# Sigmoid attention with a soft mixture of experts: logits of a whole batch in one block, a last pair by token halves, another split of held-back weights

## Chip, cores, metric

One core of a Trainium2 chip. The metric is device time in microseconds (us) of one execution, the median of several; lower is better. All data are fp32 in the chip's memory (DRAM) at the start, and the output goes back there.

## What is computed

```
scores = q @ k^T / sqrt(64) - log(448)          # 8 batches x 12 heads, 448 tokens, head size 64
x      = sigmoid(scores) @ v                    # laid out as 3584 tokens x 768
logits = x @ phi                                # 32 slots: 8 experts x 4
d      = softmax of logits over the 3584 tokens
slot   = d^T @ x                                # 32 x 768
per expert e: relu(slot[e] @ w1[e]) @ w2[e]     # 768 -> 1024 -> 768
out    = softmax of logits over the 32 slots, @ slot_out
```

The softmax over tokens runs across all batches, so it is kept as a running maximum and sum, and the slot sums are rescaled as batches come in.

## The kernel before

**Pairs and groups.** Two heads that share 128 partitions are a pair (48 pairs, `NP`); two pairs are a group (24 groups, `NG`); three groups are a batch (`NQ`). The loop `for n in range(NG)` handles one group. The engines TensorE (PE), VectorE (DVE), ScalarE (ACT) and the DMA queue SP are in manual order: each runs its instructions exactly as the program is written, and an instruction that waits holds up all that stand behind it on its engine.

**A group on PE.** `qk_full` makes the scores of both pairs for the first 384 keys in three chunks each, ACT takes the sigmoid (`sigmoid`), `av_full` multiplies by V (six matmuls per pair, two heads side by side), then come the last 64 keys of both pairs (`qk_mid` of the *next* group, `av_mid` of this one). At the start of the next group `evac` copies the result from PSUM (bank pair 2) to an x tile in SBUF. There are two x tiles, used in turn.

**Logits.** For a group, `logits_job` multiplies the two pairs of the *previous* group by phi: 4 token blocks (128, 128, 96 and 96 tokens) on 4 column quarters of the array, 8 matmuls, accumulated over two pairs. DVE adds the result to `lt_all[:, b]` (`logits_add`). So a batch has three such blocks of 8 matmuls on PE. In the group with n % 3 == 0 from n = 3 on (`edge`) the block stands between the V products of the two pairs, and the softmax over tokens of the finished batch follows (`softmax_a`, `softmax_b`). In the next group (`after`) the weights `dr` that the slot sums need are spread over partitions through DRAM: DVE transposes, SP writes `zd` and reads it back as four parts `dr` (`spread`), and on PE the block of logits is followed by `slot_job`, 56 matmuls that read `dr` part by part.

**Weights.** 128 units of 384 KB (64 of w1, then 64 of w2) stream through a ring of `N_A + N_B` = 68 SBUF tiles. `N_A` = 50 tiles (`wa`) exist from the start, and are filled during attention. The other 18 (`wb`) lie where attention's tiles were, so their loads stand behind the last attention loads on SP and wait tile by tile for what lay there. All later loads reuse ring tiles.

**The last group** (`final`) has its own order: V products of the first pair, a matmul by the identity that brings `lt_all[:, 7]` into PSUM, logits of the 4 earlier pairs so far missing there (two of them), `av_mid`, V products of the last pair, logits of the two last pairs, then `last_job`.

**The experts.** For w1: `w1_part`, `h_part`; for w2 two halves of the output columns. While the second half's products run, `out_batch` makes the outputs of the first half. `N_LATE` = 16 units are held back and loaded between the stores of the first four batches (`N_MIX` = 4 times: 4 stores, then 4 units); the other stores follow all loads. After the last unit come `gather`, `sum_groups` and the second half's `out_batch`.

**Fillers.** At the start PE runs `FILL` = 37 tiny matmuls (32x8) and `WARM` = 3 of 128x128 while the first inputs load; in the second half of w2 `warm(3)` stands in four of the steps.

Of the kernel before, what the change touches and what calls it, by code (L numbers as in the profile page):

```python
# [9 lines left out]
F32 = mybir.dt.float32  # L10
F32R = mybir.dt.float32r
AF = mybir.ActivationFunctionType
ALU = mybir.AluOpType
# [3 lines left out]
B, H, S, D = 8, 12, 448, 64  # L17
# [7 lines left out]
NFC = F // P  # L25
HALF = DM // 2
UNIT = 768
GAP = 128
N_A = 50
N_B = 18  # L30
N_LATE = 16
N_MIX = 4
QW = 2 * S
NP = B * NPR
NG = B * NQ
WARM = 3
FILL = 37
WN = 128
CW = 256
NBK = 4  # L40
# [8 lines left out]
def soft_moe_attention(ctx: ExitStack, tc: tile.TileContext, qk, v, phi, w1, w2, cst, out):  # L49
# [19 lines left out]
    nc.vector.memset(acc[:, 0:256], 0.0)  # L69
    nc.vector.memset(nbias, -math.log(S))  # L70
    nc.gpsimd.memset(lt_all, NEG)

    units = [("w1", e, 2 * uu + y, kh) for e in range(E) for uu in range(2) for kh in range(2) for y in range(2)]
    units += [("w2", hf, e, g, y) for hf in range(2) for e in range(E) for g in range(2) for y in range(2)]
# [42 lines left out]
    with ExitStack() as actx:  # L117
        ldq = actx.enter_context(tc.tile_pool(name="ldq", bufs=2))
        sp = actx.enter_context(tc.tile_pool(name="sp", bufs=2))
        one = {}  # L120
        for name in ("v0", "att4", "x0", "att3", "v2", "att0", "att1", "att2", "v1", "gap"):
            one[name] = actx.enter_context(tc.tile_pool(name=f"{name}p", bufs=1))
        yp = actx.enter_context(tc.tile_pool(name="yp", bufs=1))
        one["x1"] = actx.enter_context(tc.tile_pool(name="x1p", bufs=1))
        one["gap"].tile([P, GAP], F32, name="gap")
        bounce = actx.enter_context(tc.tile_pool(name="bounce", bufs=2, space=bass.MemoryType.DRAM))
        ps = actx.enter_context(tc.tile_pool(name="ps", bufs=1, space=PSUM))

        def bank2(i):
            return ps.tile([P, 2, 512], F32, name=f"b{i}")  # L130
# [68 lines left out]
        def av_mid(n, flags):  # L199
            att, vt = atts["mid", n], vs[n, 2]  # L200
            for h, d in enumerate(heads):
                for i, r in enumerate(heads):
                    start, stop = flags[i]
                    nc.tensor.matmul(avs["p", 2 * n + i][d, 0:S], vt[r, 0, d], att[r, h, :], start=start, stop=stop)  # L204

        def new_x(n):
            xTs[n] = one[f"x{n % 2}"].tile([P, 2, S], F32, name=f"x{n % 2}")
            for i in range(2):
                xTs["p", 2 * n + i] = xTs[n][:, i, :]

# [10 lines left out]
        def logits_job(lp, pairs, first=True, last=True):  # L221
            for m, p in enumerate(pairs):
                for j in reversed(range(4)):
                    nc.tensor.matmul(  # L224
                        lp[32 * j:32 * j + 32, 0:TOK[j]], phi_sb[:, p % NPR, :],
                        xTs["p", p][:, TOF[j]:TOF[j] + TOK[j]],
                        start=(first and m == 0), stop=(last and m == len(pairs) - 1))

        def logits_add(lp, b, first):
            for r, w in ((slice(0, 64), TOK[0]), (slice(64, 128), TOK[3])):  # L230
                dst, part = lt_all[r, b, 0:w], lp[r, 0:w]
                if first:
                    nc.vector.tensor_copy(dst, part)
                else:
                    nc.vector.tensor_tensor(out=dst, in0=part, in1=dst, op=ALU.add)

        def logits(n, i):
            lp = bank2(i)[:, 0, :]
            logits_job(lp, (2 * n, 2 * n + 1))
            return lp  # L240

        def softmax_a(b):
            t1 = small.tile([P, 2, 132], F32, name="t1")
# [183 lines left out]
        for n in range(NG):  # L427
            pa, pb = 2 * n, 2 * n + 1
            bp = n // NQ - 1
            edge, after, third = (n >= NQ and n % NQ == i for i in range(3))  # L430
            final = n == NG - 1
            if third:
                load_v(n, 1)
            load_qk(pa + 2)
            load_qk(pb + 2)
            load_v(n, 2)
            if third:
                slot_evac(bp)
            if n > 0:
                evac(n - 1)  # L440
                for p in ((pa - 4, pa - 3) if third else ()) + (() if after else (pa - 2, pa - 1)):
                    turn(p)
            if after:
                softmax_r(bp)
                softmax_c(bp)
                spread(bp)
            for _ in range(weights_of(n)):
                load_unit()
            load_v(n + 1, 0)
            if not after:  # L450
                load_v(n + 1, 1)
            if third:
                combine_c(bp)
            if edge and bp > 0 or final:
                bq = bp if final else bp - 1
                combine_d(bq, dts[bq][:, 0, 0:P])
            qk_full(pa)
            split_all(pa + 2)
            qk_full(pb)
            split_all(pb + 2)  # L460
            if final:
                avs["p", pa] = bank2(2)[:, 0, :]
                av_full(pa, True, False)
                lg = bank2(0)[:, 0, 0:P]
                nc.tensor.matmul(lg, ident, lt_all[:, B - 1], start=True, stop=False)
                logits_job(lg, [NP - 4, NP - 3], first=False, last=False)
                avs["p", pb] = bank2(3)[:, 0, :]
                av_mid(n, ((False, True), (True, False)))
                new_x(n)
                xa, xb = xTs["p", pa], xTs["p", pb]  # L470
                nc.vector.tensor_copy(xa, avs["p", pa][:, 0:S])
                turn(pa)
                av_full(pb, False, True)
                logits_job(lg, [pa], first=False, last=False)
                nc.scalar.copy(xb[:, 256:S], avs["p", pb][:, 256:S])
                nc.vector.tensor_copy(xb[:, 0:256], avs["p", pb][:, 0:256])
                logits_job(lg, [pb], first=False)
                turn(pb)
                break
            avs[n] = bank2(2)  # L480
            for i in range(2):
                avs["p", pa + i] = avs[n][:, i, :]
            av_full(pa, True, False)
            if edge:
                lp = logits(n - 1, 3)
                logits_add(lp, bp, False)
                softmax_a(bp)
                softmax_b(bp)
            av_full(pb, True, False)
            if n > 0 and not edge:  # L490
                lp = logits(n - 1, 3 if after else 0)
                if after:
                    combine_b(bp)
                logits_add(lp, n // NQ, n % NQ == 1)
            if after:
                slot_job(bp)
            qk_mid(n + 1)
            av_mid(n, ((False, True), (False, True)))
# [127 lines left out]
    for i in range(2 * E):  # L626
        w2_step(po, 1, *divmod(i, 2))
        if i == 1:
            st = sum_groups(so)
        if 3 <= i < 3 + B:  # L630
            out_batch(0, i - 3, st)
            if i < 3 + N_MIX:
                store(4)
                for _ in range(N_LATE // N_MIX):
                    load_unit()
        if 2 + B <= i < 2 * E - 2:
            warm(3)
    so = gather(po)
    store(len(stores))
    st = sum_groups(so)  # L640
# [38 lines left out]
```

## Time and profile before

| what | value |
|---|---|
| time, median of 3 runs | 391.31 us (391.17 to 393.25) |
| the profiled execution | 390.81 us, of which span 389.0 us |
| granted TensorE clock, mean | 0.985 |
| busy: DVE, ACT, POOL | 58%, 49%, 1% of the span |
| share of PE in the chain that ended last | 85% |
| share of DMA in that chain | 9% |
| read from DRAM, written | 85.43 MB, 11.47 MB |

A profile is of one execution, from its first to its last instruction (the span); the time measured contains 1.8 us around it. Busy shares are means over stages with different limits, so each stage has to be read by itself: the page's slices and the stretches (windows) do that. The chain is followed back from the last instruction, at each step to what released it. The SP rows are the DMA queue: the time at which it issued a transfer, not the transfer's end.

### The profile page before, as it was taken

How to read it: one execution, taken by the hardware profiler on the slowest of the kernel's cores; microseconds unless marked ns; L12 is line 12 of the kernel's file. 1: busy time of each engine (PE TensorE's matmuls, PEld its weight loads, DVE VectorE, ACT ScalarE, POOL GpSimd, SP SyncE). 2: the span in 40 equal slices, each digit the busy share in tenths (PEclk: the TensorE clock that was granted, in tenths of full speed). 3: DMA queues.
4: the chain of work that ended last, by engine and by line, in shares of the span. 5: the costliest groups of instructions: out<-in, count | busy, mean ns of one | idle time of the engine just before them, and what ended most of it. 6: DMA issues, size and time to landing. Idle time of an engine off the chain costs nothing.

```text
span 389.0 us, 9831 instructions
## 1 busy us (share of the span) xinstructions
PE 364.2 (94%) x4058; PEld 188.8 (49%) x4058; DVE 226.5 (58%) x518; ACT 190.2 (49%) x243; POOL 3.3 (1%) x13
## 2 busy tenths in 40 slices
PE   8999999999999999999999999999989989977750
PEld 5444556554555654555554456555455543313210
DVE  3555776776887677697667777776643410420340
ACT  4656675664667456566645666564530110320240
POOL 1000000000000000000000000000020000000000
PEclk9999999999999999999999999999999999999995
DMA  7777856773784567477547755442899999999987
GB/s 212 256 245 238 285 156 192 244 255 102 244 296 144 183 227 239 161 240 244 195 137 227 274 159 203 142 150 70 294 390 387 401 399 402 383 385 374 366 287 242
DMA packets 49276, 97.54 MB, mean 251 GB/s; under 512 B 5584, under 2 KB 26704, under 8 KB 49232
## 3 DMA queue, kind: packets, MB, share of 16 engines
q1 hardware_dynamic: 49232, 96.92, 72.7%
q8 instruction: 32, 0.52, 0.6%
q14 instruction: 12, 0.10, 0.1%
HBM read 85.43 MB, written 11.47 MB: 249 GB/s over the span
## 4 chain that ended last, share of the span: by engine, by line
PE 85%; DMA 9%; DVE 2%; ACT 1%; issue 1%; SPq 0%; ACTq 0%
PE b L195 29%; PE b L176 24%; PE b L187 6%; PE px L535 6%; PE b L204 5%; DMA wb<-in_w_dram 4%; PE b L318 4%; DMA wa<-in_w_dram 3%; PE b L224 3%; PE po L601 3%; PE px L578 2%; PE px L552 1%; DMA qkt<-in_qk_dram 1%; DVE wa L583 1%; PE b L383 0%
## 5 line engine op out<-in xcount | busy, mean ns | idle before, releaser
L164 ACT ACTIVATE att<-b,nbias 128x896 f32<-128x896 f32 x168 | 158.6, 1007 | 84.7 <-PE b L187 64.7
L195 PE MATMUL b<-att,v 128*64 128x448 f32 x576 | 115.3, 545 | 0.0
L176 PE MATMUL b<-qs,ks 64*128 64x448 f32 x864 | 95.7, 372 | 0.0
L176 PEld LDWEIGHTS b<-qs,ks 64*128 64x128 f32 x864 | 77.4, 184 | 26.3 <-PE b L187 6.3
L195 PEld LDWEIGHTS b<-att,v 128*64 128x64 f32 x576 | 38.5, 136 | 61.6 <-issue 54.1
L213 DVE COPY x<-b 128x896 f32<-128x896 f32 x23 | 25.1, 1091 | 33.1 <-PE b L204 33.1
L155 DVE TENSOR_TENSOR qs<-qkt,qs 128x448 fp32r<-128x448 f32 x48 | 30.0, 625 | 1.7
L155 DVE TENSOR_TENSOR ks<-qkt,ks 128x384 fp32r<-128x384 f32 x48 | 26.8, 558 | 1.6
L219 DVE STREAM_TRANSPOSE y<-x 128x448 f32<-128x448 f32 x48 | 27.3, 617 | 0.4
L187 PE MATMUL b<-qkt 64*64 64x448 f32 x192 | 25.2, 569 | 0.3 <-DMA qkt<-in_qk_dram 0.2
L153 DVE CAST qs<-qkt 128x448 fp32r<-128x448 f32 x48 | 18.4, 384 | 9.6 <-DMA qkt<-in_qk_dram 6.5
L204 PE MATMUL b<-att,v 64*64 64x448 f32 x192 | 22.4, 537 | 0.0
L583 DVE COPY wa<-px 96x768 f32<-96x768 f32 x13 | 12.2, 952 | 13.2 <-PE px L578 13.2
L583 ACT COPY wa<-px 128x768 f32<-128x768 f32 x13 | 10.3, 799 | 17.6 <-PE px L578 14.2
L535 PE MATMUL px<-wa,sT 128*32 128x256 f32 x300 | 17.8, 381 | 0.6 <-DVE sT L386 0.6
L578 PE MATMUL px<-st,lt_all 32*128 32x384 f32 (+1 forms) x128 | 16.8, 524 | 1.5 <-DVE st L614 0.7
L318 PE MATMUL b<-y,dr 32*32 32x192 f32 x896 | 17.7, 331 | 0.2 <-ACT dr L309 0.2
L224 PEld LDWEIGHTS b<-x,phit 128*32 128x32 f32 x384 | 9.1, 109 | 17.0 <-issue 11.3
L153 DVE CAST ks<-qkt 128x384 fp32r<-128x384 f32 x47 | 16.6, 353 | 0.0
L224 PE MATMUL b<-x,phit 128*32 128x96 f32 (+1 forms) x384 | 16.0, 266 | 0.2
L614 DVE COPY st<-px 128x384 f32<-128x384 f32 x2 | 1.1, 557 | 25.4 <-PE px L612 25.4
L318 PEld LDWEIGHTS b<-y,dr 32*32 32x32 f32 x896 | 12.9, 103 | 3.4 <-issue 1.4
(131 smaller groups left out, 211.5 us busy)
## 6 DMA issues: line engine op xcount, KB each, us to landing
wa<-in_w_dram SPq DMA_DIRECT2D x98, 384.0 KB, 7.0
qkt<-in_qk_dram SPq DMA_DIRECT2D x48, 448.0 KB, 4.1
wb<-in_w_dram SPq DMA_DIRECT2D x30, 384.0 KB, 5.8
v<-in_v_dram SPq DMA_DIRECT2D x48, 192.0 KB, 2.5
out_dram<-wa SPq DMA_DIRECT2D x26, 192.0 KB, 3.4
out_dram<-wa SPq DMA_DIRECT2D x26, 144.0 KB, 3.2
dr<-zd SPq DMA_DIRECT2D x28, 64.0 KB, 2.0
v<-in_v_dram SPq DMA_DIRECT2D x24, 64.0 KB, 4.2
```

The lines of the kernel that those rows point to most:

```text
L153: copy(dst[:, 0, :], src)
L155: nc.vector.tensor_tensor(out=dst[:, 1, :], in0=src, in1=dst[:, 0, :].bitcast(F32), op=ALU.subtract)
L164: nc.scalar.activation(att[:], sc[:, :, 0:S], AF.Sigmoid, bias=nbias, scale=QSCALE)
L176: nc.tensor.matmul(sc[:, h, 0:S], ks[r, z, c * P:(c + 1) * P], qs[r, y, :], start=(z + y == 0), stop=(z == 1))
L187: nc.tensor.matmul(sc[r, h, 0:S], t[d, S + NQK:QW], t[d, 0:S], start=True, stop=True)
L195: nc.tensor.matmul(avs["p", p][r, 0:S], vs[n, i][:, c, r], atts[p, c][:, h, :], start=(start and c == 0), stop=(stop and c == NFULL - 1))
L204: nc.tensor.matmul(avs["p", 2 * n + i][d, 0:S], vt[r, 0, d], att[r, h, :], start=start, stop=stop)
L219: nc.vector.transpose(ys[b][:, hp, :], xTs["p", p])
L224: nc.tensor.matmul(lp[32 * j:32 * j + 32, 0:TOK[j]], phi_sb[:, p % NPR, :], xTs["p", p][:, TOF[j]:TOF[j] + TOK[j]], start=(first and m == ...
L318: nc.tensor.matmul(sl[a // 2][32 * j:32 * j + 32, a % 2, 0:NPR * BLK], drs[b][32 * a:32 * a + 32, j, c * BLK:(c + 1) * BLK], y[32 * a:32 * ...
L535: nc.tensor.matmul(ph[32 * j:32 * j + 32, uu, 0:256], sT[:, 3 * kh + kc, :], utile[("w1", e, 2 * uu + j // 2, kh)][:, kc * 256:(kc + 1) * ...
L583: (nc.scalar.copy if g == 0 else nc.vector.tensor_copy)(ov, pf[g][0:n, :, 0:HALF])
```

## The change

Five edits:

1. Logits of a batch are computed in one block of 24 matmuls (six pairs, accumulated in PSUM) in the `edge` group, and copied once by DVE (`logits_copy` for `logits_add`). The two other blocks of each batch go. Since x must live for three groups there are three x tiles; the tile `gap` goes, and one tile moves from `wa` to `wb` (`N_A` 49, `N_B` 19). For the last batch `lt_all[:, 7]` is set to 0 (tokens) by POOL instead of holding sums, and the final group computes the logits of four earlier pairs instead of two.
2. In the final group the V products of the last pair are made for tokens 0 to 255 and 256 to 447 apart, in two PSUM banks, each copied to x by its own engine (DVE, ACT).
3. `N_LATE` is 12: four times 4 stores and 3 units.
4. `FILL` 42 and `WARM` 6 at the start.
5. Seven tiny matmuls behind each `warm(3)` in the second half of w2.

```
-N_A = 50
-N_B = 18
-N_LATE = 16
+N_A = 49
+N_B = 19
+N_LATE = 12
-WARM = 3
-FILL = 37
+WARM = 6
+FILL = 42
...
+    for r, w in ((slice(0, 64), TOK[0]), (slice(64, 128), TOK[3])):
+        nc.gpsimd.memset(lt_all[r, B - 1, 0:w], 0.0)
...
         def new_x(n):
-            xTs[n] = one[f"x{n % 2}"].tile([P, 2, S], F32, name=f"x{n % 2}")
+            xTs[n] = one[f"x{n % NQ}"].tile([P, 2, S], F32, name=f"x{n % NQ}")
...
+        def logits_copy(lp, b):
             for r, w in ((slice(0, 64), TOK[0]), (slice(64, 128), TOK[3])):
+                nc.vector.tensor_copy(lt_all[r, b, 0:w], lp[r, 0:w])
...
-                logits_job(lg, [NP - 4, NP - 3], first=False, last=False)
-                avs["p", pb] = bank2(3)[:, 0, :]
-                av_mid(n, ((False, True), (True, False)))
+                logits_job(lg, range(NP - NPR, NP - 2), first=False, last=False)
+                halves = ((0, 256), (256, S))
+                ab = bank2(3)
+                for h, d in enumerate(heads):
+                    for i, r in enumerate(heads):
+                        lhs, att = vs[n, 2][r, 0, d], atts["mid", n]
+                        if i == 0:
+                            nc.tensor.matmul(avs["p", pa][d, 0:S], lhs, att[r, h, :], start=False, stop=True)
+                        else:
+                            for z, (lo, hi) in enumerate(halves):
+                                nc.tensor.matmul(ab[d, z, 0:hi - lo], lhs, att[r, h, lo:hi], start=True, stop=False)
...
-                av_full(pb, False, True)
+                for z, (lo, hi) in enumerate(halves):
+                    for c in range(NFULL):
+                        for h, r in enumerate(heads):
+                            nc.tensor.matmul(
+                                ab[r, z, 0:hi - lo], vs[n, 1][:, c, r], atts[pb, c][:, h, lo:hi],
+                                start=False, stop=(c == NFULL - 1))
                 logits_job(lg, [pa], first=False, last=False)
-                nc.scalar.copy(xb[:, 256:S], avs["p", pb][:, 256:S])
-                nc.vector.tensor_copy(xb[:, 0:256], avs["p", pb][:, 0:256])
+                for (lo, hi), copy, z in zip(halves, (nc.vector.tensor_copy, nc.scalar.copy), range(2)):
+                    copy(xb[:, lo:hi], ab[:, z, 0:hi - lo])
...
             if edge:
-                lp = logits(n - 1, 3)
-                logits_add(lp, bp, False)
+                lp = bank2(3)[:, 0, :]
+                logits_job(lp, range(2 * (n - NQ), 2 * n))
+                logits_copy(lp, bp)
                 softmax_a(bp)
                 softmax_b(bp)
             av_full(pb, True, False)
-            if n > 0 and not edge:
-                lp = logits(n - 1, 3 if after else 0)
-                if after:
-                    combine_b(bp)
-                logits_add(lp, n // NQ, n % NQ == 1)
+            if after:
+                combine_b(bp)
...
             warm(3)
+            for j in range(7):
+                r = slice(j % 4 * 32, j % 4 * 32 + 32)
+                nc.tensor.matmul(wt[r, 0:8], ident[r, 0:32], ident[r, 0:8], start=True, stop=True)
```

Three places show how instructions move. In the order's rows stand the line, the operation, what it writes and reads (`b` are PSUM bank pairs, numbers tell one use from the next) and the shape; line numbers differ between the two kernels (L318 of before is L309 of the change, L93 is L94, L592 is L594).

PE in group 4, an `after` group, from the V products of its second pair to the slot sums. Before:

```order
L195 MATMUL b_761<-att_744,v_566 64x448 x2
L195 MATMUL b_761<-att_753,v_566 64x448 x2
L224 MATMUL b_774<-x_680,phit 32x96 x2
L224 MATMUL b_774<-x_680,phit 32x128 x2
L224 MATMUL b_774<-x_680,phit 32x96 x2
L224 MATMUL b_774<-x_680,phit 32x128 x2
L318 MATMUL b_791<-y,dr 32x192 x8
L318 MATMUL b_792<-y,dr 32x192 x8
```

The same place in the change:

```order
L195 MATMUL b_764<-att_738,v_553 64x448 x2
L195 MATMUL b_764<-att_747,v_553 64x448 x2
L195 MATMUL b_764<-att_756,v_553 64x448 x2
L309 MATMUL b_783<-y,dr 32x192 x8
L309 MATMUL b_784<-y,dr 32x192 x8
```

The four rows of logits have gone, and the slot sums stand directly behind the V products.

PE in group 3, an `edge` group, the logits between the V products of its two pairs. Before:

```order
L195 MATMUL b_634<-att_593,v_441 64x448 x2
L224 MATMUL b_641<-x_552,phit 32x96 x2
L224 MATMUL b_641<-x_552,phit 32x128 x2
L224 MATMUL b_641<-x_552,phit 32x96 x2
L224 MATMUL b_641<-x_552,phit 32x128 x2
L195 MATMUL b_634<-att_608,v_443 64x448 x2
```

The end of that place in the change (two rows like the first two stand ahead of them):

```order
L224 MATMUL b_628<-x_318,phit 32x96 x2
L224 MATMUL b_628<-x_318,phit 32x128 x2
L224 MATMUL b_628<-x_429,phit 32x96 x2
L224 MATMUL b_628<-x_429,phit 32x128 x2
L224 MATMUL b_628<-x_429,phit 32x96 x2
L224 MATMUL b_628<-x_429,phit 32x128 x2
L224 MATMUL b_628<-x_539,phit 32x96 x2
L224 MATMUL b_628<-x_539,phit 32x128 x2
L224 MATMUL b_628<-x_539,phit 32x96 x2
L224 MATMUL b_628<-x_539,phit 32x128 x2
L195 MATMUL b_621<-att_595,v_441 64x448 x2
```

One block now reads three x tiles and writes one bank, 24 matmuls instead of 8.

SP at the first stores of the output. Before:

```order
L93 DMA wa_4174<-in_w_dram 128x768
L592 DMA out_dram<-wa_4381 128x384 x2
L592 DMA out_dram<-wa_4383 96x384 x2
L93 DMA wa_4389<-in_w_dram 128x768
L93 DMA wa_4391<-in_w_dram 128x768
L93 DMA wa_4393<-in_w_dram 128x768
L93 DMA wa_4395<-in_w_dram 128x768
L592 DMA out_dram<-wb_4407 128x384 x2
```

The same place in the change:

```order
L94 DMA wa_4166<-in_w_dram 128x768
L594 DMA out_dram<-wa_4361 128x384 x2
L594 DMA out_dram<-wb_4363 96x384 x2
L94 DMA wb_4369<-in_w_dram 128x768
L94 DMA wb_4371<-in_w_dram 128x768
L94 DMA wb_4373<-in_w_dram 128x768
L594 DMA out_dram<-wb_4385 128x384 x2
```

Four units more stand ahead of the first store, and three instead of four between stores.

## Rows read from the trace of the kernel before

**Rows 1.** The page: busy time of engines; DMA and GB/s in 40 slices of 9.7 us.

```profile
PE 364.2 (94%) x4058; PEld 188.8 (49%) x4058; DVE 226.5 (58%) x518; ACT 190.2 (49%) x243; POOL 3.3 (1%) x13
...
DMA  7777856773784567477547755442899999999987
GB/s 212 256 245 238 285 156 192 244 255 102 244 296 144 183 227 239 161 240 244 195 137 227 274 159 203 142 150 70 294 390 387 401 399 402 383 385 374 366 287 242
```

**Rows 2.** The chain that ended last, in time: start us, us, engine, name, line.

```profile
15.55 0.91 PE b L187 x8
...
45.15 0.57 PE b L224 x14
...
53.72 4.66 PE b L195 x24
...
58.95 2.13 PE b L318 x95
...
93.67 2.13 PE b L318 x94
...
128.47 2.13 PE b L318 x95
...
163.20 2.13 PE b L318 x95
...
282.27 0.44 DVE x L476
...
296.68 2.73 PE px L535 x48
...
356.62 5.47 DMA wb<-in_w_dram
```

**Rows 3.** Timeline of the SP queue, 262 us to the end: start us, us, line, transfer, count.

```profile
264.84 6.79 SPq L145 DMA_DIRECT2D v<-in_v_dram  x3
271.68 17.81 SPq L93 DMA_DIRECT2D wb<-in_w_dram  x18
...
291.88 39.88 SPq L93 DMA_DIRECT2D wa<-in_w_dram  x42
...
357.39 28.00 SPq L592 DMA_DIRECT2D out_dram<-wa  x48
```

**Rows 4.** Waits of the SP queue, 268 to 300 us: total, times, longest.

```profile
SPq L145 <- PE b L204: 3.7, 1, 3.7
```

**Rows 5.** Stretches: length, busy PE, PEld, DVE, ACT, POOL, granted clock, DMA share, GB/s.

```profile
54.00:55.00 1.00, 1.00 (x8) 0.43 (x6) 0.97 (x3) 0.62 (x2) 0.00 (x0) 1.00 0.05 11
...
270.00:272.00 2.00, 2.00 (x24) 1.04 (x18) 1.38 (x3) 1.01 (x1) 0.00 (x0) 1.00 0.00 0
...
332.00:334.00 2.00, 2.00 (x24) 0.46 (x16) 0.58 (x1) 0.64 (x1) 0.00 (x0) 1.00 1.03 401
```

**Rows 6.** Timeline of the SP queue, the reads of dr of the first four batches.

```profile
55.71 1.75 SPq L295 DMA_DIRECT2D dr<-zd  x4
...
90.56 1.75 SPq L295 DMA_DIRECT2D dr<-zd  x4
...
125.08 1.75 SPq L295 DMA_DIRECT2D dr<-zd  x4
...
158.77 1.75 SPq L295 DMA_DIRECT2D dr<-zd  x4
```

**Rows 7.** Lines L295 (reads of dr, 28) and L292 (writes of zd, 7): issue to landing.

```profile
DMA to landing us min/median/max: 1.8/2.0/2.7
...
DMA to landing us min/median/max: 1.5/1.7/3.0
```

**Rows 8.** Timeline of PE, first 7 us.

```profile
2.35 1.65 PE L417 MATMUL b<-acc 128*128 128x128 f32 x6
4.16 1.67 PE L187 MATMUL b<-qkt 64*64 64x448 f32 x4 [0.17 <-DMA qkt<-in_qk_dram]
5.98 0.97 PE L187 MATMUL b<-qkt 64*64 64x448 f32 x4
```

More of the change, by code (lines that the diff above doesn't have):

```diff
@@ L27 @@
 UNIT = 768
-GAP = 128
-N_A = 50
-N_B = 18
-N_LATE = 16
+N_A = 49
+N_B = 19
+N_LATE = 12
 N_MIX = 4
@@ L120, in soft_moe_attention @@
         one = {}
-        for name in ("v0", "att4", "x0", "att3", "v2", "att0", "att1", "att2", "v1", "gap"):
+        for name in ("v0", "att4", "x0", "x1", "att3", "v2", "att0", "att1", "att2", "v1"):
             one[name] = actx.enter_context(tc.tile_pool(name=f"{name}p", bufs=1))
         yp = actx.enter_context(tc.tile_pool(name="yp", bufs=1))
-        one["x1"] = actx.enter_context(tc.tile_pool(name="x1p", bufs=1))
-        one["gap"].tile([P, GAP], F32, name="gap")
+        one["x2"] = actx.enter_context(tc.tile_pool(name="x2p", bufs=1))
         bounce = actx.enter_context(tc.tile_pool(name="bounce", bufs=2, space=bass.MemoryType.DRAM))
@@ L227, in logits_job @@
                         start=(first and m == 0), stop=(last and m == len(pairs) - 1))
-        def logits_add(lp, b, first):
+        def logits_copy(lp, b):
             for r, w in ((slice(0, 64), TOK[0]), (slice(64, 128), TOK[3])):
[L231 to L240, printed above, removed]
+                nc.vector.tensor_copy(lt_all[r, b, 0:w], lp[r, 0:w])
         def softmax_a(b):
```

## Prediction, made before the changed kernel was run

> **What bounds the kernel now.** I read the page first [rows 1]: PE is busy for 94% of the span, and the DMA line stays between 2 and 8 tenths up to 282 us and reads 9 in every slice after that but the last two. So there are two stages with two limits. The chain shows the first: until about 282 us it lies on PE alone, group after group, with no gap between pieces. Four kinds of piece matter here [rows 2]: the V products of a group (4.66), a block of logits (0.57), the slot sums (2.13) and `qk_mid` (0.91). Whatever PE is spared there, the stage is shorter by.
>
> The second limit is seen on the SP queue [rows 3]. Its last three attention loads take from 264.84 to 271.6, because the one for the last 64 keys waits 3.7 us for `av_mid` of group 22 (line L204) [rows 4]; from 270 to 272 the DMA engines move nothing [rows 5]. At 271.68 the first `wb` unit follows, and from then on transfers queue: 42 units are issued in 39.88 us, 0.95 us each, at a DMA share of 1.03 [rows 3, 5]. The last unit lands at 362.1 (356.62 + 5.47) [rows 2], and the 48 stores left at 357.39 are issued over 28.00 us up to 385.4 [rows 3]. So the end is the moment at which PE frees SP in group 22, plus what has to be moved after it. A gain on PE ahead of that moment counts in full, one behind it only if DMA runs dry, and a unit more behind it costs a unit.
>
> **Logits in one block.** A block alone takes 0.57 [rows 2]. The price of 16 more matmuls in an existing block is not in the trace. The nearest row is w1 [rows 2]: 48 instructions in 2.73 us, four side by side, with the same 128 x 32 weights, are 12 steps of 256 columns, 0.228 each, or 0.114 per 128 columns. (A matmul is two instructions here.) A pair of logits is two such steps, so the four added pairs cost 8 x 0.114 = 0.91. The V products give nearly the same: 24 instructions, two side by side, are 12 steps of 448 columns in 4.66, 0.111 per 128. Up to `av_mid` of group 22 the change removes 15 blocks (14 in batches 0 to 6, one in group 22), 15 x 0.57 = 8.55, and adds 7 x 0.91 = 6.37: **2.2 us less on PE**. Bounds: 0.6 if an added pair costs what it costs in a block of its own (0.285, so 1.14 per edge), 2.4 by the V products' price. I take the w1 price because its tile is the same. The DVE additions saved lie beside PE and are worth nothing; the third x tile frees no one, as no row shows PE waiting for x.
>
> **A wait that comes closer.** In an `after` group the block removed stood ahead of the slot sums, which need `dr`. The way to `dr` (`av_mid` of the group before, DVE, the write of `zd`, the four reads) hangs on the start of the group and does not move with the block. The four reads are issued in 1.75 us, the last 1.31 after the first, and land 2.0 later [rows 6, 7]: in the first batch at 59.0, when the slot sums began at 58.95; in the second at 93.9 against 93.67; in the third at 128.4 against 128.47; in the fourth at 162.1 against 163.20 [rows 2], and the three that follow lie like the fourth. With PE 0.57 earlier the fourth part is 0.6, 0.8 and 0.5 late in the first three, and in time in the others. How much lateness is free? In the second batch it was 0.2 late, and the slot sums took 2.13 as elsewhere; at an even pace the 13th of 56 matmuls, the first that needs the fourth part, would be due after 12/56 x 2.13 = 0.46. So the three waits cost between 0.5 (late minus 0.46) and 1.3 (late minus 0.2). I take the middle, **0.9 us more**. Behind a waiting slot sum stand `qk_mid`, `av_mid` and the whole next group, so it counts in full.
>
> Why the first three are later is in the write of `zd`: issue to landing takes 1.5 at least, 1.7 in the median, 3.0 at most [rows 7]. While the slowest was under way the DMA share fell to 0.05 [rows 5], so a full queue does not explain it. The Trainium skill, page "DMA: Bandwidth & Descriptors", section "Latency and other measured facts", has it that the fixed cost of a transfer is mostly the memory's answer, and smaller when memory is lightly loaded; by that rule all seven writes should be near the short value, as load was light, and the wait would be nothing, not 0.9. The row speaks against it for three of seven.
>
> **The start.** Five tiny matmuls add about 0.16 (74 instructions take the 1.17 us ahead of 2.35, so 37 matmuls at 0.032). The three 128 x 128 ones take 1.81 up to the start of `qk_mid` at 4.16, at the slower pace: the first half of `qk_mid` takes 1.67, the second, 1.8 later, 0.97 [rows 8]. Three more are about 1.3, for six instructions at twice the 0.111 above. So the first half of `qk_mid` begins at 5.5 instead of 4.16. It had slack: its second half waits until 5.98 for the second input. Eight such matmuls together take 0.91 in a later group [rows 2], no more than four alone, so the remainder of the first half can run beside the second. I take **0.1 more**. Bounds: 0, and 1.1 if the first half keeps its slow pace to the end (5.5 + 1.67 = 7.2, then 0.97, against 6.95 now).
>
> **One unit more after the free moment.** 49 instead of 50 units are loaded in attention, so 79 follow. At 0.95 each [rows 3]: **0.95 more**; between 0, if the early part of the tail has a gap that it fills, and 1.1. I take 0.95, since the DMA line reads 9 in nearly every slice of the tail [rows 1].
>
> **Twelve held back.** From 331.8 on (291.88 + 39.88) [rows 3] SP waited a while for the first output tile; but DMA stood at 1.03 from 332 to 334 [rows 5], on what was queued. Four more units there fill a gap of the queue, not of the engines. Ahead of the last unit still stand the same 16 stores, and 48 behind it: **0**. If the cover were gone (a drained queue), those 2 us would count, as a gain.
>
> **The final group.** Two more pairs of logits (0.46), six more weight loads for the halves (0 to 0.3), against a copy of 0.44 on DVE that so far ran after ACT's [rows 2] and now runs beside the second half: about +0.2 on PE. It is hidden: SP has 15 `wb` units to load at that time, now 16, and only the three in y wait for the slot sums. **0**, at most 0.3. The fillers in w2 stand where PE waits for units: **0**.
>
> **Sum.** -2.2 + 0.9 + 0.1 + 0.95 = -0.25 us. The profiled execution took 390.81 (span 389.0 and 1.8 around it), 0.5 less than the median of the runs, 391.31. Against the profile that is 390.6, against the median **391.1**, which is my forecast: no change. About 0.5%, 2 us, is what a measurement of this kernel can tell from none: faster means under 389.35, slower over 393.27.
>
> **Rivals.**
> 1. *No wait for dr.* The writes of `zd` all land near 1.5, as four of seven do. For it: the slow ones are the first three, which may be chance. Against: three in a row. The gain of 2.2 stays but for the start and the unit: -1.15, 390.2.
> 2. *The tail gives back the unit as well.* The queue is not full in its first microseconds, so the added unit, whose space is free before y, might fill a hole there. With no dr wait either: -2.1, 389.2, just faster. Against: share 1 and more from there on.
> 3. *The removed block turns into a wait in every batch*, slower than before. Place: the slot sums in the seven `after` groups. If all writes of `zd` take the 3.0 of the slowest, the fourth part lands at 163.6 in the fourth batch, where PE asks from 162.6 on: 1.0 late, 0.5 to 0.8 of cost, and three more like it, 2.6 together. With the 0.9 that makes 3.5, so +2.35, 393.7. From a sum of waits of 1.15 on the kernel is slower than before, from 3.1 on measurably. For it: the row with 3.0. Against: the last four writes were short.
> 4. *The start loses 1.1*, all else as forecast: 392.1.
> 5. *The halves do not do what they say*: the copy of the first half waits for the whole bank pair, as one tile. Then the final group is 0.4 longer, still under cover: 391.1, in the forecast.
>
> **How the numbers follow.** Forecast with rival 5: 0.50. Rival 1: 0.20. Rival 2: 0.13. Rival 3: 0.10. Rival 4: 0.07. Faster is rival 2 and a tail of rival 1: 0.15. Slower is rival 3 and a little of rival 4: 0.11. The rest, 0.74, is within 0.5%. The range goes from rival 2 to rival 4 with what the bounds of the unit and the waits add: 389.1 to 392.9; it leaves out rival 3 and some of the ends.
>
> **What would show it.** Right: blocks of logits of about 1.5 us at the edges in the chain and none elsewhere; `av_mid` of group 22 ending some 1.2 earlier, near 270; pieces of the slot sums longer than 2.13, or a gap ahead, in the first three batches alone; the first scores near 7.0; the last unit landing 0.2 to 0.4 earlier than 362.1 and 27 us from there to the end. Wrong: the first `wb` unit at 269.4 or sooner (rival 1), or the last unit landing by more than 1 earlier than before (rival 2); slot sums with waits in all batches (rival 3); a DMA share well under 1 between 285 and 360, which would break the rule that the tail moves with its start.

## Result and profile after

| | before | changed |
|---|---|---|
| median of 22 runs, side by side | 391.45 us (389.90 to 396.42) | 393.52 us (390.17 to 397.05) |
| ratio | | 1.0044, 95% interval 1.0027 to 1.0062 |
| profiled execution | 390.81 us | 397.05 us |

The change costs 1.7 us (1.1 to 2.4): nearly the 0.5% that counts as a difference here, and 0.6 us above the predicted range. The profiled execution of the changed kernel, 3.5 us longer than its median, counts as a slow one and is left out of the ratio, so what is read from it is compared below with a second one of the same kernel (392.78 us).

The page, in the form of [rows 1], with the clock line:

```profile
PE 372.5 (94%) x4146; PEld 195.7 (50%) x4146; DVE 219.4 (56%) x488; ACT 190.2 (48%) x243; POOL 3.7 (1%) x15
...
PEclk9999999999999999999999999999989999999555
DMA  6777756673785676378467634354989999999797
GB/s 208 221 260 254 273 156 223 219 238 100 253 283 160 201 236 249 91 254 283 159 200 237 253 87 174 121 165 160 334 340 362 403 401 401 386 320 389 270 311 236
```

The tail's DMA line no longer reads 9 throughout. Its first 8 there is the slice from 286 to 296 us, where the clock line has its first 8 too. (The clock of 5 in the last slices is in this execution and, in part, in those of `u_tiny`, `b_shift` and `e_shift` below; in the second execution of the changed kernel it is in the last slice alone, as before.)

The chain [rows 2]: the blocks of logits and two slot sums.

```profile
45.21 1.45 PE b L224 x42
...
59.34 2.15 PE b L309 x101
...
94.98 1.74 PE b L309 x82
```

A block of six pairs takes 1.45; the prediction had 0.57 + 0.91 = 1.48. Only one of the seven slot sums waited noticeably for `dr`: the second, whose fourth part landed at 94.94 with the sums begun at 93.81.

The SP queue [rows 3] and its waits from 268 to 300 us [rows 4]:

```profile
265.16 6.19 SPq L145 DMA_DIRECT2D v<-in_v_dram  x3
271.40 19.20 SPq L94 DMA_DIRECT2D wb<-in_w_dram  x19
294.39 45.11 SPq L94 DMA_DIRECT2D wa<-in_w_dram  x48
...
361.42 30.15 SPq L594 DMA_DIRECT2D out_dram<-wa  x48
```

```profile
SPq L94 <- PE px L537: 6.0, 6, 3.8
```

The `wb` units start 0.28 earlier than before, at 271.40, and are issued by 290.6. Then come 3.8 us until the first reload of a `wa` tile, which waits for w1 (L537) to be done with it. The kernel before has this wait too, but of 1.5 us; it is in the view of [rows 4]:

```profile
SPq L93 <- PE px L535: 2.2, 4, 1.5
```

There that reload was issued at 290.98; now at 294.39. What held up w1 is on PE (columns: start us, us, engine, line, operation, names, shapes, count, idle before and what ended it):

```profile
288.32 0.53 PE L374 MATMUL b<-acc,t 128*32 128x192 f32 x8
288.75 0.51 PE L374 MATMUL b<-x,t 128*32 128x192 f32 x2
291.25 0.65 PE L374 MATMUL b<-x,t 128*32 128x192 f32 x6 [1.99 <-issue]
292.47 2.69 PE L537 MATMUL px<-wa,sT 128*32 128x256 f32 x24 [0.57 <-DVE sT L377]
```

The sixteen matmul instructions that combine the slots stop after the tenth for 1.99 us, "issue": no semaphore in the profile released it. In the kernel before the same place runs without a stop:

```profile
288.11 0.53 PE L383 MATMUL b<-acc,t 128*32 128x192 f32 x8
288.53 0.82 PE L383 MATMUL b<-x,t 128*32 128x192 f32 x8
289.92 1.50 PE L535 MATMUL px<-wa,sT 128*32 128x256 f32 x24 [0.58 <-DVE sT L386]
291.36 0.27 PE L396 MATMUL px<-cw,csb 128*128 128x1 f32 x1
291.91 0.16 PE L396 MATMUL px<-cw,csb 128*128 128x1 f32 x1 [0.28 <-issue]
```

There is a stop here too, of 0.28, but 25 instructions into w1 (in `finish`, L396). Around the stop one transfer of another queue passes; the DMA view of the changed kernel from 288 to 290 us (packets, MB, share of 16 engines):

```profile
q1 hardware_dynamic: 284, 0.78, 99.3%
q8 instruction: 1, 0.02, 3.4%
```

It is a packet of 16 KB on the instruction queue q8, from 288.67 to 289.76 in the trace. The matmul behind the stop starts at 291.25. And PE's matmul instructions counted from the start of the program (from 0) give the place its name: **it is number 3254 in the changed kernel and number 3253 in the kernel before**. The stop lies at a fixed place of the instruction stream, and the program has been moved under it.

What followed, in stretches (columns as in [rows 5]), of the changed kernel and then of the kernel before:

```profile
290.00:295.00 5.00, 3.18 (x30) 1.27 (x30) 0.93 (x4) 0.00 (x0) 0.81 (x4) 0.66 0.82 315
295.00:300.00 5.00, 5.00 (x82) 2.95 (x78) 1.07 (x3) 0.00 (x0) 0.00 (x0) 1.00 0.86 286
```

```profile
290.00:295.00 5.00, 4.72 (x82) 2.85 (x85) 1.43 (x5) 0.00 (x0) 0.60 (x3) 1.00 1.00 377
295.00:300.00 5.00, 5.00 (x83) 2.76 (x76) 0.85 (x2) 0.42 (x2) 0.00 (x0) 1.00 1.01 387
```

DMA moved 62 and 101 GB/s less for 5 us each: 0.82 MB, or two units of 0.39 MB, worth 2 us at 0.95 each. The granted clock also fell after the stop (mean 0.66, between its two levels of 1.2 and 2.4 GHz), so the first 24 instructions of w1 took 2.69 instead of 1.50. The last unit lands at 367.25 in this execution, 362.09 before.

### The profile page after: what moved, and what is told of

The parts are those of the page before. It is cut to its first block, busy times and chain, and to the rows that moved or that the text cites. A ratio compares the mean times of both kernels' runs of the same rounds, so it can differ in the third digit from the quotient of the medians.

```text
span 395.2 us, 9983 instructions
## 1 busy us (share of the span) xinstructions
PE 372.5 (94%) x4146; PEld 195.7 (50%) x4146; DVE 219.4 (56%) x488; ACT 190.2 (48%) x243; POOL 3.7 (1%) x15
## 4 chain that ended last, share of the span: by engine, by line
PE 78%; DMA 16%; DVE 1%; issue 1%; SPq 1%; ACT 1%; ACTq 0%
PE b L195 27%; PE b L176 23%; DMA wa<-in_w_dram 10%; PE b L187 6%; PE b L204 4%; PE b L309 4%; PE px L580 3%; PE px L537 3%; PE b L224 3%; DMA out_dram<-wb 3%; DMA wb<-in_w_dram 2%; PE b L408 1%; DMA dr<-zd 1%; DMA zd<-t 1%; PE po L603 1%
## 5 line engine op out<-in xcount | busy, mean ns | idle before, releaser
L195 PE MATMUL b<-att,v 128*64 128x448 f32 x564 | 112.8, 545 | 0.0
L195 PEld LDWEIGHTS b<-att,v 128*64 128x64 f32 x564 | 37.7, 136 | 59.9 <-issue 52.5
L580 PE MATMUL px<-st,lt_all 32*128 32x384 f32 (+1 forms) x128 | 20.9, 684 | 0.9 <-DVE st L616 0.7
L204 PE MATMUL b<-att,v 64*64 64x448 f32 x184 | 21.4, 536 | 0.0
L537 PE MATMUL px<-wa,sT 128*32 128x256 f32 x294 | 19.0, 400 | 0.6 <-DVE sT L377 0.6
L309 PE MATMUL b<-y,dr 32*32 32x192 f32 x896 | 17.9, 331 | 0.7 <-DMA dr<-zd 0.5
L585 DVE COPY wa<-px 96x768 f32<-96x768 f32 x12 | 11.4, 954 | 12.8 <-PE px L580 9.9
L331 DVE SCALAR_TENSOR_TENSOR acc<-acc,t,b 128x384 f32<-128x384 f32 x12 | 6.8, 611 | 17.6 <-PE b L309 17.6
L309 PEld LDWEIGHTS b<-y,dr 32*32 32x32 f32 x896 | 12.6, 103 | 8.0 <-issue 4.9
L580 PEld LDWEIGHTS px<-st,lt_all 32*128 32x128 f32 (+1 forms) x128 | 8.0, 221 | 14.4 <-issue 5.0
```

Of the source, the lines that this page charges most:

```text
L195: nc.tensor.matmul(avs["p", p][r, 0:S], vs[n, i][:, c, r], atts[p, c][:, h, :], start=(start and c == 0), stop=(stop and c == NFULL - 1))
L309: nc.tensor.matmul(sl[a // 2][32 * j:32 * j + 32, a % 2, 0:NPR * BLK], drs[b][32 * a:32 * a + 32, j, c * BLK:(c + 1) * BLK], y[32 * a:32 * ...
L537: nc.tensor.matmul(ph[32 * j:32 * j + 32, uu, 0:256], sT[:, 3 * kh + kc, :], utile[("w1", e, 2 * uu + j // 2, kh)][:, kc * 256:(kc + 1) * ...
L580: nc.tensor.matmul(pf[j // 2][0:TOK[j], j % 2, 0:HALF], lt_all[r, b, 0:TOK[j]], st[r, :], start=True, stop=True)
```

## Experiments

Ratios are against the kernel before on the same chip, 12 runs beside 35 (median of the 35: 391.61 us for the `u_` runs, 391.86 for `e_shift` to `c_all`, 391.99 for the last four). The ratio on record is not the quotient of the two medians: they differ by up to 0.24% (`only_logits`: 2.3 us faster by the ratio, 1.3 by the medians), so differences of 1 us between programs are not to be read from one of them alone. Theories: **A** the longer warm-up at the start costs; **C** the 12 held back units cost in the tail; **D** the halves of the last pair disturb what follows; **E** the tiny matmuls in w2; and, from the second group of runs on, **F** the place in PE's instruction stream.

### One part undone at a time

`u_start`: start as before.

```
-WARM = 6
-FILL = 42
+WARM = 3
+FILL = 37
```

> The change with the start of the kernel before (3 large and 37 tiny matmuls). Theory A (the longer warm-up is what costs: in the trace of the changed kernel the first scores begin at 7.98 us instead of 6.95, since all four products of the first qk_mid kept 1.6 us instead of two of them): first scores near 6.95, 1.0 us below the changed kernel, 0.7 us above the kernel before (ratio 1.002). Theory B (the start is taken up by a later wait for a transfer, and the loss arises in the tail): first scores near 6.95 all the same, but the time stays within 0.3 us of the changed kernel (ratio 1.004).

390.68 us, ratio 0.9969 (0.9943 to 0.9995): 2.8 us below the changed kernel, more than theory A allows, and faster than before.

`u_late`: `N_LATE = 16`.

> The change with 16 units held back. Theory A (the loss is the start's): as the changed kernel, ratio 1.004, and the end as late after the last unit as there. Theory C (the tail: with 3 units between the stores instead of 4 the last unit lands later and TensorE's granted clock falls before the outputs of the second half, 12.1 us for them instead of 10.7): the time falls by 1 to 2 us, to a ratio of 0.999 to 1.002, and from the landing of the last unit to the end it is 27 us again instead of 27.9.

392.43 us, 1.0028 (1.0002 to 1.0054). The interval overlaps that of the changed kernel; the stop is there, 1.70 long.

`u_half`: the V products of the last pair as before (`av_mid` for both pairs, `av_full(pb, False, True)`, two copies from one bank).

> The change with the last pair's V products in one piece, as before. Theory A or C: as the changed kernel within 0.3 us (ratio 1.004). Theory D (the halves disturb last_job: in the profiled execution of the changed kernel TensorE stood still for 1.99 us inside the ten combining matmuls at 289.3 us, which the kernel before did not): no such stop, and 1 to 2 us below the changed kernel. If the stop comes and goes between executions without this edit, it belongs to the single execution and not to the halves.

391.61 us, 0.9978 (0.9953 to 1.0004): 1.9 us below the changed kernel, and no stop in the combination. That read like theory D, but this edit also takes 16 matmul instructions out of the stream ahead of that place, exactly as many as `u_start` does. In both the stop has moved to the tenth instruction of w1: number 3253.

`u_tiny`: the loop of seven tiny matmuls in w2 taken out.

> The change without the seven tiny matmuls in four steps of the second half of w2. Theory A, C or D: as the changed kernel within 0.3 us (ratio 1.004), the steps of w2 wait for their units with or without them. Theory E (the tiny matmuls hold up the steps, or lower the granted clock in the stretch behind the last unit): 0.5 to 1.5 us below the changed kernel.

393.58 us, 1.0057 (1.0027 to 1.0087): no gain. The stop is at number 3254, 2.58 long. E falls.

So the programs with the stream ahead of the combination as in the changed kernel (that kernel, `u_late`, `u_tiny`) keep the stop there, and two edits that have nothing to do with each other take it away, with the time. That made theory F. (The expectations call a matmul instruction a pass: a matmul is two.)

### The instruction stream alone

`e_shift`: the changed kernel with eight tiny matmuls (16 instructions) fewer; warm-up, halves and the 12 units stay.

```
-FILL = 42
+FILL = 34
```

> The changed kernel with 34 tiny matmuls at the start instead of 42, nothing else; the 6 large ones, the halves and the 12 held back units stay. Theory F (in the profiles of the changed kernel and of two of its variants TensorE stands still for 1.7 to 2.6 us at one and the same matmul of its stream, right behind the 16 KB transfer of the instruction queue at 287 to 290 us, and in these programs that matmul lies inside the sixteen that combine the slots; 16 passes fewer ahead of it, and it lies 9 passes into w1, where the weights in reach cover it): combining takes 1.24 us without a stop, the DMA queue has no hole at 291 to 299 us, time 390.7 to 391.7, ratio 0.998 to 1.001. Theories A and D (start or halves, both kept here): the stop may move, but the time stays at 393.3 (ratio 1.004).

390.90 us, **0.9958** (0.9937 to 0.9980): the time is within what F said, the ratio below its 0.998 to 1.001, which the interval just touches; A and D had 1.004. PE and the stretches:

```profile
286.37 0.53 PE L374 MATMUL b<-acc,t 128*32 128x192 f32 x8
286.79 0.81 PE L374 MATMUL b<-x,t 128*32 128x192 f32 x8
288.18 0.81 PE L537 MATMUL px<-wa,sT 128*32 128x256 f32 x9 [0.58 <-DVE sT L377]
290.13 1.07 PE L537 MATMUL px<-wa,sT 128*32 128x256 f32 x15 [1.14 <-issue]
```

```profile
290.00:295.00 5.00, 4.87 (x85) 2.92 (x88) 1.08 (x3) 0.00 (x0) 0.00 (x0) 1.00 0.96 355
295.00:300.00 5.00, 5.00 (x80) 2.76 (x76) 1.11 (x4) 0.60 (x3) 0.00 (x0) 1.00 1.02 384
```

The combination runs through, nine instructions of w1 follow, and the stop of 1.14 leaves a small hole in DMA: 0.96 where the changed kernel has 0.82.

`b_shift`: the kernel before, with the stream moved the other way.

```
             nc.tensor.matmul(pa[0:1, 0, 0:P], m1[:, 1:2], ident, start=True, stop=True)
-            warm(2)
+            for j in range(18):
+                r = slice(j % 4 * 32, j % 4 * 32 + 32)
+                nc.tensor.matmul(pw[r, 0:8], ident[r, 0:32], ident[r, 0:8], start=True, stop=True)
```

> The kernel before, with the second pair of 128x128 warming matmuls in last_job replaced by 18 tiny ones of 32x8 at the same spot (a stretch in which TensorE waits for the softmax): 32 passes more in the stream and about as much time. Theory F: the same matmul of the stream now lies inside the combination of the slots as in the changed kernel, a stop of about 2 us there, weights for the ring issued 2 us later, 1.5 to 2.5 us slower than the kernel before (ratio 1.004 to 1.006) with nothing else of the change in it. Theories A and D: no change (ratio 1.000).

394.26 us, **1.0049** (1.0025 to 1.0074): 1.9 us slower, with nothing of the change in it. PE, the SP queue and the stretches:

```profile
288.32 0.53 PE L385 MATMUL b<-acc,t 128*32 128x192 f32 x8
288.73 0.51 PE L385 MATMUL b<-x,t 128*32 128x192 f32 x2
290.94 0.53 PE L385 MATMUL b<-x,t 128*32 128x192 f32 x6 [1.70 <-issue]
292.05 1.50 PE L537 MATMUL px<-wa,sT 128*32 128x256 f32 x24 [0.58 <-DVE sT L388]
```

```profile
272.10 18.29 SPq L93 DMA_DIRECT2D wb<-in_w_dram  x18
293.10 40.27 SPq L93 DMA_DIRECT2D wa<-in_w_dram  x44
```

```profile
290.00:295.00 5.00, 3.48 (x56) 2.04 (x59) 1.25 (x6) 0.00 (x0) 0.81 (x4) 1.00 0.86 306
295.00:300.00 5.00, 5.00 (x92) 2.88 (x88) 1.60 (x3) 0.42 (x2) 0.00 (x0) 1.00 0.93 292
```

The stop lands after the tenth of the sixteen, number 3254, as in the changed kernel. DMA misses 71 and 95 GB/s against the kernel before, 0.83 MB or two units again. The clock stayed at 1.00 around the stop here, so the fall after it in the changed kernel's profile is not needed for the hole. It fell later, from 365 to 375 us, where it was 1.00 in the kernel before; in this execution 2.4 us are lost up to the landing of the last unit (counted as in the table below), and 0.7 from there to the end (27.63 against 26.93).

`only_logits`: the changed kernel with start, last pair, `N_LATE` and w2 as before.

> Of the change the logits in one block alone (with its three x tiles, 49 and 19 ring tiles and the four pairs in the last group); start, last pair, 16 held back units and w2 as before. By the sum of the prediction without the start: logits 2.2 us less, one unit more 0.95, so 390.2 without a dr wait (ratio 0.997), 391.1 with 0.9 of it (ratio 0.999). Theory F adds: w1 begins at the same place of the instruction stream relative to the block of instructions as in the kernel before (25 passes ahead of it), so no stop of over 0.5 us.

390.54 us, 0.9942 (0.9916 to 0.9967): 2.3 us (1.3 to 3.3) faster. A wait for `dr` of 0.9 would have left 0.4, no wait 1.25; by the ratio it is faster than either, and why is open.

`c_all`: the changed kernel with the start of before and `N_LATE = 16`.

> The changed kernel with the start of before and 16 held back units. Theory F: 16 passes fewer, no stop in the combination, 390.7 us as with the start alone (ratio 0.998); if the 12 units also cost in the tail (theory C), up to 1 us below that (ratio 0.995). If the start alone does it without F, the same numbers: this run tells the number of held back units, at a start that is known.

390.70 us, 0.9958 (0.9938 to 0.9978); `u_start`, with 12, has 390.68 on another chip, and `e_shift`, with 12, 0.9958 on the same. The number held back makes no difference that shows. Its profiled execution has a hole in DMA without a stop in the combination:

```profile
290.00:295.00 5.00, 4.59 (x80) 2.71 (x82) 1.07 (x3) 0.00 (x0) 0.00 (x0) 1.00 0.82 286
```

### The changed kernel again, and the terms left over

`again`: no edit.

> The changed kernel once more, as it is, beside the next three on one chip. Theory F: a stop of 1.5 to 2.6 us at the tenth of the sixteen combining matmuls in this execution too, ratio 1.003 to 1.006. If the stop is absent and the time is as high all the same, F is not what makes it slower. First scores between 6.4 and 8.1 us, as in the other executions with either start.

393.40 us, 1.0031 (1.0007 to 1.0056). The stop is in this execution too, 2.04 long, and so is the late reload (the rest of w1's start at the lower clock, 24 instructions in 2.61):

```profile
286.72 0.51 PE L374 MATMUL b<-x,t 128*32 128x192 f32 x2
289.28 0.53 PE L374 MATMUL b<-x,t 128*32 128x192 f32 x6 [2.04 <-issue]
290.39 2.61 PE L537 MATMUL px<-wa,sT 128*32 128x256 f32 x24 [0.59 <-DVE sT L377]
```

```profile
269.41 19.29 SPq L94 DMA_DIRECT2D wb<-in_w_dram  x19
292.09 44.27 SPq L94 DMA_DIRECT2D wa<-in_w_dram  x48
```

`only_unit`: the kernel before with `N_A = 49`, `N_B = 19` and `GAP = 896`.

> The kernel before with one ring tile moved from the first to the second kind (49 and 19), the room taken by a larger unused tile; nothing else, and TensorE's stream of instructions is the same to the last one. The sum of the prediction: one unit more to land behind the free moment, 0.95 us slower (ratio 1.0024). If another limit stands there, 0 (ratio 1.000).

392.70 us, 1.0011 (0.9986 to 1.0036), or +0.4 us (-0.5 to 1.4): it does not tell 0.95 from 0.

`s_half`: the changed kernel with start and last pair of before; 12 units and the tiny matmuls stay.

> The changed kernel with the start and the last pair of before; 12 held back units and the seven tiny matmuls per step stay. It differs from the run with the logits alone by these two only, and both have the block of instructions end 25 passes into w1. Prediction: both cost nothing, ratio 0.994 to 0.997 as with the logits alone. Theory C: the 12 units cost 0.5 to 1.5 us in the tail, ratio 0.998 or more.

390.23 us, 0.9959 (0.9929 to 0.9989). Beside `only_logits` no cost of the two shows.

`best2`: `only_logits` with the stop moved on to instruction 57 of w1.

```
-WARM = 3
-FILL = 37
+WARM = 4
+FILL = 20
```

> The logits alone, with 4 large and 20 tiny matmuls at the start instead of 3 and 37: 32 passes fewer, so that the stop falls 57 passes into w1, with the start as long as before (2.7 against 2.9 us of fillers). Theory F: no more to be had, since the 0.68 us left of the stop at 25 passes made no hole in the DMA queue: ratio 0.994 to 0.996. If even that stop costs, another 0.3 to 0.7 us less (ratio 0.993).

390.81 us, 0.9983 (0.9957 to 1.0008). No stop of 0.25 or more is left at the start of w1, and no more is gained: the expectation, 0.994 to 0.996, is missed: it came out slower. That it is worse than `only_logits` can't be said: the intervals overlap.

### All executions side by side

"Stop": where instruction 3253 or 3254 lies, and how long PE stood there. "Reload": from the first combining matmul to the issue of the first `wa` reload. "Landing": from the end of the last group's scores to the landing of the last unit. us, one profiled execution each.

| program | stop at | stop | reload | landing | ratio of the runs |
|---|---|---|---|---|---|
| before | w1, 25 | 0.28 | 2.87 | 86.94 | 1 |
| `only_unit` | w1, 25 | 0.76 | 2.87 | 87.79 | 1.0011 |
| `b_shift` | combination, 10 | 1.70 | 4.78 | 89.37 | 1.0049 |
| `best2` | w1, 57 | none | 2.87 | 87.87 | 0.9983 |
| `s_half` | w1, 25 | 0.68 | 2.87 | 87.40 | 0.9959 |
| `only_logits` | w1, 25 | 0.68 | 2.87 | 87.52 | 0.9942 |
| `e_shift` | w1, 9 | 1.14 | 4.16 | 88.86 | 0.9958 |
| `u_start` | w1, 9 | 1.34 | 4.37 | 88.39 | 0.9969 |
| `u_half` | w1, 9 | 1.49 | 4.72 | 91.45 | 0.9978 |
| `c_all` | w1, 9 | 1.89 | 4.92 | 89.75 | 0.9958 |
| `u_late` | combination, 10 | 1.70 | 5.72 | 90.33 | 1.0028 |
| `again` | combination, 10 | 2.04 | 5.79 | 90.32 | 1.0031 |
| changed | combination, 10 | 1.99 | 6.07 | 92.34 | 1.0044 |
| `u_tiny` | combination, 10 | 2.58 | 6.54 | 92.79 | 1.0057 |

From the top of the new programs (`best2`) down, the later the reload the later the landing, mostly about one for one: 2.9 us more reload from `only_logits` to `again`, 2.8 us more to the landing. Three executions (`u_half`, the changed kernel, `u_tiny`) lose some 2 us more in the last part of the tail, where units and stores alternate; why is not settled, and it isn't in `again`. All programs with the stop in the combination are slower than the kernel before, and no other is by more than its interval.

The times do not follow the reload as evenly as the landings do. The four programs with the stop nine instructions into w1 ran at 0.9958 to 0.9978, the three new ones with it later at 0.9942 to 0.9983, though the profiled executions of the four land 0.5 to 4 us later. `c_all` has a reload of 4.92 and the hole shown above, and is no slower than `s_half` without either; `b_shift`, with 4.78, lost 1.9 us. So the runs show that the place of the stop costs or saves the time. That the late reload and the hole are the link is read from one execution of each program, and is not shown.

## Why the prediction was wrong

**The step that failed** is the final group: "It is hidden: SP has 15 `wb` units to load at that time, now 16, and only the three in y wait for the slot sums. 0, at most 0.3." The cover was not there. The `wb` units are all issued when the combination is barely over (289.5 in the kernel before, whose combination ends at 289.35; 290.6 in the changed kernel, during its stop), and the next transfer on SP needs a tile that w1 must have read. The kernel before already waits 1.5 us there (`SPq L93 <- PE px L535` above), in the same view from which [rows 4] show another wait. So PE's time from the slot sums to the first instructions of w1 decides when that transfer starts. And the instructions that the change adds were counted as PE time only (five tiny matmuls 0.16, three large ones 1.3, six more weight loads), not as 32 more places in PE's instruction stream: 16 at the start, and the other 16 in the halves. (The 16 for two more pairs of logits stand against 16 removed with group 22's block.) They bring the stop from w1's 26th instruction, where 0.28 us of it showed, to the middle of the combination, where it is 1.7 to 2.6. `b_shift` prices that alone at 1.9 us (1.0 to 2.9); from the changed kernel to `e_shift` it is 2.5 to 2.6 by the medians. The other row of the kernel before that could have told is in PE's timeline, shown above: 0.28 "issue" in front of L396, a stop without a waiter.

The other steps, by the prediction's order:

- **Logits, -2.2: right.** 1.45 per edge block. From the first scores to the end of the last group's scores, three executions with the old blocks took 268.27, 268.65 and 269.60, eleven with the new 265.77 to 268.38, median 266.31: 2.3 less, with all waits in it. (The bound of 2.4 by the V products' price is 2.3: 8.55 less 56 x 0.111.)
- **A wait for dr, +0.9: too much in most executions.** Three batches were to pay; in the changed kernel's profiled execution one paid, 0.7, and the others next to nothing. Over the eleven executions with the new logits the seven slot sums together are 0 to 0.7 us longer than undisturbed, 0.2 in the median. `only_logits` agrees with rival 1, no wait (-1.25 without the start), better than with the forecast, by the medians (-1.3) and by the ratio (-2.3). The step that fell is that the parts come 0.5 late in the third batch: there the fourth part landed at 128.43 and the sums began at 129.01. The prediction also had the last three batches lie like the fourth, whose fourth part is in time by 0.8 in the kernel before; in the sixth and seventh it is by 0.4. The prediction set the rule of the Trainium skill (page "DMA: Bandwidth & Descriptors", section "Latency and other measured facts") against three late rows; as a forecast "no wait" came out nearer. The writes themselves do not bear that rule out: in the changed kernel the first two still took 2.52 and 2.55, the other five 1.52 to 1.73.
- **The start, +0.1: no cost shows.** The changed kernel's first scores stand at 7.91 instead of 6.88, which is rival 4's picture, but that is the single execution: with 6 large matmuls five other executions or variants have 6.45 to 7.11, and with 3 they reach from 6.17 to 8.09 (seven executions, mean 7.07; the six with 6 have a mean of 7.0). Beside a scatter of 2 us, 0.1 can't be told from 0.
- **One unit more, +0.95: open.** 0.4 (-0.5 to 1.4), with the landing 0.85 later in the one profile.
- **12 held back, 0, and the tiny matmuls, 0: right** as far as the runs resolve (`c_all`, `s_half`, `u_tiny`).
- **The halves, 0: right, by rival 5.** DVE's copy of the first half begins only when the last product of the second is done, so nothing runs beside anything. From the last scores to the combination it takes 13.39 to 13.42 with or without halves, 12.96 in the kernel before: the 0.4 are the two more pairs.

DVE in the changed kernel; the last product on L475 starts at 281.8:

```profile
282.14 0.42 DVE L480 COPY x<-b 128x256 f32<-128x256 f32 x1 [1.11 <-PE b L475]
```

Without the missed term the sum stands: -2.3 for logits and waits, 0 to 0.1 for the start, 0.4 to 0.95 for the unit give -1.9 to -1.25. The seven programs with the change's logits and no stop in the combination (`u_start`, `u_half`, `e_shift`, `c_all`, `s_half`, `only_logits`, `best2`) ran at 0.9942 to 0.9983, 0.7 to 2.3 us faster, around that sum. So two terms erred in opposite directions: a wait of 0.9 that was mostly not there, and a stop of 1.9 to 2.6 that was not in the sum. That the forecast of no change is off by no more than 2.4 us is in part luck. The warning the prediction gave ("a DMA share well under 1 between 285 and 360") is the sign that came true, at 290 to 300.

## To carry over

On an engine with thousands of instructions, "issue" gaps without a waiter can sit at a fixed number in the stream: count instructions up to the gap in each version before blaming the edit nearest to it, and test with a few idle instructions added or removed far ahead of it. An edit that looks free (fillers, one matmul split in two) moves all places behind it; a place for such a stop is where the engine waits anyway, or where transfers are queued deep enough. And a queue is only as covered as its next transfer: ask what frees the first tile after the units now in line.

## What was not expected of the hardware

During the execution packets of 16 KB arrive on an instruction queue, q8: 32 within the changed kernel's span, one per 127 of its matmul instructions in the mean, and one per 126 in the kernel before. They are read here as PE's instructions, since the stop lies right behind one in every execution where it shows; no run tests it. Thirteen of the fourteen executions show matmul 3253 or 3254 starting 2.30 to 2.57 us after the start of such a packet (in `best2`, where PE has other work up to there, 3.20), although the packet itself takes only 1.0 to 1.1. The reading is that PE, where it has less than that left to do, stands still for the rest. It fits that 24 V products in attention take 4.66 us and no stop of 0.25 us without a waiter shows there; in the last slot sums and the combination 112 and 16 instructions take 2.35 and 1.24 in the kernel before, and there it does. Why the stop varies from 1.1 to 2.6 us at equal places, and whether the full DMA queue (share 0.99 around the packet) lengthens it, was not tried.

The Trainium skill, page "Trainium Architecture — The Big Picture", section "The software stack", gives an instruction 64 bytes; by that a packet would hold 256, or 128 matmuls with a weight load each (an estimate), and the 126 and 127 found agree. The same section has the instruction streams put into each engine's memory when the program is loaded; the packets seen during the execution do not fit with that as the whole of it, and the measurement decides.
